# A mask of scores as four 64x64 quarter products in place of 67-row products

## Chip, cores and metric

The kernel runs on one core of a Trainium2 chip. The metric is the device time in microseconds, as a median of several runs. A separate execution was recorded by the hardware profiler; all rows below come from it.

## What is computed

Three layers stand behind one another. The first is an attention with 2 batches, 8 heads, 768 positions and a head size of 64. Each query sees the keys less than 16 positions away and, with `log(32)` added to the score, 24 summaries, each the maximum of k (mean of v) over a block of 32 positions:

```python
scores_s = scale * einsum(q, k_sum) + log(32)
scores_l = where(abs(i - j) < 16, scale * q @ k.T, -1e9)
a = softmax(concat([scores_l, scores_s]))
x = a @ concat([v, v_sum])
```

The second is a gated layer: `h = relu(x @ w_in)`, a convolution of three taps along the positions, `h * sigmoid(conv) @ w_out`. The third normalises x and adds `relu(xn @ w_ch1) @ w_ch2` to it. The weights arrive as 64-bit floats and are narrowed on the chip into a high and a low part.

## The kernel before, in words

All work is cut into named steps (`plan.op`), 1850 of them. A long list at the head of the file (`ORDER`) gives the order in which they are issued and the engine of each; each engine works through its own steps in that order, so a step that waits holds up what stands behind it on its engine.

The attention goes by pairs of blocks of 64 queries: `pair(j)`, j from 0 to 11, six per batch. A pair holds 8 heads as two units u = 2j and 2j + 1 (heads in the lower and the upper half of the partitions). Each unit has one PSUM bank of 128 queries (two blocks of 64) by four heads by 120 keys: 24 summaries and a window of 96 positions (16 ahead of the block, its 64, 16 behind it). The steps of a pair in order:

- `M{u}` (L460 to L466) takes a bank and writes the additive mask into it, as a product of `mask_l` and `mask_r`, with 480 columns (four heads of 120). `mask_l` (L293) holds the identity of 64 rows twice side by side, and three rows of ones; `mask_r` (L303) holds 64 rows of window masks in three variants (first block of a batch, middle, last block) and three rows that add up to `log(32)` under the summaries. Where both blocks of the pair use the same variant, it is one product of 67 rows by 128 queries; otherwise two of 67 rows by 64 queries.
- `S{j}` (L468 to L476) adds the scores: 32 products of 64x64 tiles with 120 columns, for four heads p, two units a and two blocks h_.
- `X`, `E`, `Q`, `R`, `N` (maximum, exponential, reciprocal, scaling), `P` (transposes back), `C` (copy) and `T` (product with the windows of v, L480). `H` and `L` split the result into high and low parts for the next layer.

Banks of the attention come from a ring of five. The steps `h` (L704) and `x` (L778) are the second layer, `ch` (L1114) and `ac` (L1149) the third; from about 49 us on the steps of the second layer stand among the pairs of the attention.

On TensorE the order around the masks is M1, M3, M0, S0, M2, S1 for pairs 0 and 1; then M4, M5, S2; M7, M6, S3; M9, M8, S4; M10, M11, S5; M15, M13, M14, M12, S6, S7; M17, M16, S8; M19, M18, S9; M20, M21, S10; M23, M22, S11. Between the masks of one pair no other step of TensorE stands, but for pairs 0 and 1 and pairs 6 and 7, which are interleaved as shown.

On GpSimd the order at the start is: `mhalf` (L319), `mask_r`, the identity `ident` (L282, used by every transpose and by the first steps of TensorE at L358), a clearing of `kw` (L322) and of `vw` (L594), `ind` (L284), a clearing of `xT`, `mask_l`, and then copies of k (L395). All loads go through one queue, SyncE's.

Of the kernel before, what the change touches and what calls it, by code (L numbers as in the profile page):

```python
# [100 lines left out]
F32 = mybir.dt.float32  # L101
F32R = mybir.dt.float32r
U32 = mybir.dt.uint32
BF16 = mybir.dt.bfloat16
AF = mybir.ActivationFunctionType
ALU = mybir.AluOpType
# [3 lines left out]
NEG = -1e9  # L110
F64_SCALE = 2.0 ** -112
F64_SIGN = -(2.0 ** 32)
LN32 = (3.46875, -0.003021240234375, 7.152557373046875e-06)
# [48 lines left out]
def local_summary_attention_moe_kernel(  # L162
# [26 lines left out]
    NB = S // 32  # L189
    HK = 16  # L190
    WN = 15
    K0 = NB + HK
    K1 = K0 + 64
    NK = K1 + HK
    SCALE = 1.0 / float(D) ** 0.5

    V, A, G, T = nc.vector, nc.scalar, nc.gpsimd, nc.tensor
# [7 lines left out]
    def pool(name, bufs=1, space=None, side="left"):  # L205
        kw = {} if space is None else {"space": space}
        return tc.alloc_tile_pool(name=name, bufs=bufs, side=side, **kw)

    const = pool("const")
# [4 lines left out]
    ps_a = pool("ps_a", space=PSUM, side="right")  # L214

    ident = const.tile([128, 128], F32, name="ident")
    mask_l = const.tile([67, 128], BF16, name="mask_l")
    mask_r = const.tile([67, 3, NK], BF16, name="mask_r")
    crow = const.tile([28, 128], F32, name="crow")
    ccol = const.tile([128, 28], F32, name="ccol")  # L220
    mhalf = const.tile([128, NT], F32, name="mhalf")
# [28 lines left out]
    def scaled(e, out, in_, c=None):  # L250
        if e == "A":
            A.copy(out, in_) if c is None else A.mul(out, in_, c)  # L252
        elif c is None:
            on[e].tensor_copy(out, in_)
        else:
            on[e].tensor_scalar(out=out, in0=in_, scalar1=c, scalar2=1.0, op0=ALU.mult, op1=ALU.mult)  # L256
# [3 lines left out]
    def bank(tag):  # L260
        p, n = PS[tag]
        return p.tile([128, 512], F32, tag=tag, name=tag, bufs=n)
# [27 lines left out]

    ind_op = plan.op("ind", (("G", 640),), make_ind)

    def make_mask_l(e):  # L293
        G.memset(mask_l[0:64], 0.0)
        G.affine_select(
            out=mask_l[0:64].rearrange("p (a j) -> p a j", a=2),
            in_=mask_l[0:64].rearrange("p (a j) -> p a j", a=2),
            compare_op=ALU.not_equal, fill=1.0, base=0,
            pattern=[[0, 2], [-1, 64]], channel_multiplier=1,
        )  # L300
        G.memset(mask_l[64:67], 1.0)

    def make_mask_r(e):  # L303
        G.memset(mask_r, 0.0)
        loc = mask_r[0:64, :, NB:NK]
        G.affine_select(out=loc, in_=loc, compare_op=ALU.is_ge, fill=NEG, base=WN - HK,
                        pattern=[[0, 3], [1, NK - NB]], channel_multiplier=-1)
        G.affine_select(out=loc, in_=loc, compare_op=ALU.is_ge, fill=NEG, base=HK + WN,
                        pattern=[[0, 3], [-1, NK - NB]], channel_multiplier=1)
        G.memset(mask_r[0:64, 0, NB:K0], NEG)  # L310
        G.memset(mask_r[0:64, 2, K1:NK], NEG)
        ln = mask_r[64:67, :, 0:NB]
        G.memset(ln, LN32[0])
        for i in (0, 1):
            G.affine_select(out=ln, in_=ln, compare_op=ALU.is_ge, fill=LN32[i + 1], base=i,
                            pattern=[[0, 3], [0, NB]], channel_multiplier=-1)

    masks = [plan.op("mask_l", (("G", 600),), make_mask_l), plan.op("mask_r", (("G", 2354),), make_mask_r)]
    G.memset(mhalf, -0.5)  # L319
    kz = {}  # L320
# [108 lines left out]
    live = {}  # L429
# [13 lines left out]
    def pair(j):  # L443


        n, half = divmod(j, 2)
        c = n % NCH
        ws = (2 * half, 2 * half + 1)
        waits = KE[n] + [KC[n], KH[n]] + QE[n] + ([kz[n % 3]] if n % 3 in kz else [])
        if half == 0 and c > 0:  # L450
            waits.append(KX[n])
        if half == 1 and c < NCH - 1:
            waits.append(KX[n + 1])
        var = [0 if (c == 0 and w == 0) else 2 if (c == NCH - 1 and w == NW - 1) else 1 for w in ws]
        ms, cs = [], []
        for a in range(2):
            u = 2 * j + a
            tag = "tr"

            def f_m(e, u=u, tag=tag):  # L460
                sc = live["sc", u] = bank(tag)
                for h_ in range(1 if var[0] == var[1] else 2):
                    s_ = slice(0, 128) if var[0] == var[1] else slice(64 * h_, 64 * h_ + 64)
                    T.matmul(sc[s_, 0:4 * NK].rearrange("p (a c) -> p a c", a=4), mask_l[:, s_],
                             mask_r[:, var[h_]].unsqueeze(1).to_broadcast([67, 4, NK]), start=True, stop=False)
            ms.append(plan.op(f"M{u}", (("P", 200),), f_m, masks, take=[(tag, ("s", u))]))  # L466

        def f_s(e):  # L468
            for p in range(4):
                for a in range(2):  # L470
                    for h_ in range(2):
                        T.matmul(live["sc", 2 * j + a][64 * h_:64 * h_ + 64, p * NK:(p + 1) * NK],  # L472
                                 qb[n % 2][64 * a:64 * a + 64, p, ws[h_], :], kw[n % 3][64 * a:64 * a + 64, p, ws[h_], :],
                                 start=False, stop=(p == 3))

        s = S_[j] = plan.op(f"S{j}", (("P", 950),), f_s, waits + ms)  # L476
        for a in range(2):
            cs.append(unit(2 * j + a, s))

        def f_av(e):  # L480
            av = live["av", j] = bank("tr")
            ps = [live.pop(("ps", 2 * j + a)) for a in range(2)]
            for h_ in range(2):
                vv = vw[j % 3][0:NK, h_, :].rearrange("p (h e) -> p h e", h=4)
                for p in range(4):
                    for a in range(2):
                        s_ = slice(64 * a, 64 * a + 64)
                        T.matmul(av[s_, h_ * 256 + p * 64:h_ * 256 + p * 64 + 64], vv[:, p, s_],  # L488
                                 ps[a][:, p, 64 * h_:64 * h_ + 64], start=True, stop=True)

        tt = T_[j] = plan.op(f"T{j}", (("P", 1090),), f_av, cs + [LV[j], LVS[j]], take=[("tr", ("av", j))])
        for a in range(2):
            tt.give.append(("probT", 2 * j + a))
        if half == 0:
            def f_new(e):
                t = xTT[n] = m1.tile([128, 2, 4, CH + 2], F32R, tag="xT", name="xT", bufs=2)
                xT[n] = [t[:, k_] for k_ in range(2)]
                if c == 0:
                    G.memset(t[:, :, :, 0:1].bitcast(F32), 0.0)
                if c == NCH - 1:  # L500
                    G.memset(t[:, :, :, CH + 1:CH + 2].bitcast(F32), 0.0)
            XT[n] = plan.op(f"xT{n}", (("G", 100),), f_new, [], take=[("xT", n)])
        o = 1 + 128 * half
        av_ = lambda: live["av", j].rearrange("p (w h j) -> p h w j", w=2, h=4)
        to = lambda x: x[:, :, o:o + 128].rearrange("p h (w j) -> p h w j", w=2)
        XH[j] = plan.op(f"H{j}", EVAC, lambda e: scaled(e, to(xT[n][0]), av_()), [tt, XT[n]])

        def f_lo(e):
            hi, lo = xT[n]
            V.tensor_tensor(out=to(lo), in0=av_(), in1=to(hi).bitcast(F32), op=ALU.subtract)  # L510

        XL[j] = plan.op(f"L{j}", (("V", 598),), f_lo, [XH[j]])
        XL[j].give.append(("tr", ("av", j)))
        if half == 0 and c > 0:
            def f_halo(e):
                u_, d_ = xTT[n - 1], xTT[n]
                scaled(e, u_[:, :, :, CH + 1:CH + 2], d_[:, :, :, 1:2])
                scaled(e, d_[:, :, :, 0:1], u_[:, :, :, CH:CH + 1])
            HL[n] = plan.op(f"xh{n}", (("V", 200), ("G", 470)), f_halo, [XL[j], XL[j - 1]])
# [166 lines left out]
    def m_step(i):  # L686
# [84 lines left out]
        for t in range(2):  # L771
# [10 lines left out]
            if f == NF - 1:  # L782
                def fe(e, t=t):
# [10 lines left out]
                                                   in_=conv_w.rearrange("k (f p) -> (k f) p", p=256))),  # L794
# [464 lines left out]
```

## Time and profile before

| | |
|---|---|
| median of 3 runs | 496.11 us (495.74 to 496.38) |
| profiled execution, whole time | 497.45 us |
| its span, first to last instruction | 495.6 us |
| TensorE busy | 478.3 us (96%) |
| VectorE, ScalarE, GpSimd busy | 303.6, 227.7, 143.5 us |
| mask products at L464 | 32 |

The profiled execution is one of its own, with a whole time a little above its span; a sum made against it is carried over to the median of the runs as a difference. Engine names in the rows are PE (TensorE matmul), PEld (its weight loads), DVE (VectorE), ACT (ScalarE), POOL (GpSimd) and SPq (SyncE's issue of loads). A matmul's listed duration contains the filling and emptying of the array, so the pace of a run of products is read from one start to the next, not from single durations. An engine's idle time is named after what ended it, in brackets behind an arrow.

### The profile page before, as it was taken

What the parts mean: (1) busy time and instruction counts of PE and PEld (TensorE: products, weight loads), DVE (VectorE), ACT (ScalarE), POOL (GpSimd) and SP (SyncE); (2) the same over time, 40 slices, a digit from 0 to 9 for tenths busy, and PEclk for the clock granted to TensorE, in tenths of its full rate; (3) what the DMA queues carried; (4) which work ended last, traced back from release to release, by engine and by line L of the source; (5) the groups of instructions that cost most, each with busy time, mean ns of one, the idle gap of its engine ahead of it and who ended that gap; (6) DMA issues with size and microseconds to landing.
All of it is one profiled execution on the core that took longest, in us unless ns stands there. A gap on an engine that the chain in (4) does not pass through costs nothing.

```text
span 495.6 us, 8628 instructions
## 1 busy us (share of the span) xinstructions
PE 478.3 (96%) x3342; PEld 415.8 (84%) x3342; DVE 303.6 (61%) x601; ACT 227.7 (46%) x605; POOL 143.5 (29%) x177
## 2 busy tenths in 40 slices
PE   6886999999999999999999999999999999999997
PEld 4545989888888888887889989899899888989985
DVE  3888999889867898999899751304551012301114
ACT  3888986674856587745443412314342010110100
POOL 5554565554233364325323102222422000000000
PEclk9898999999999999999999999999999999999999
DMA  8999997213100423000450402113240001200003
GB/s 267 346 246 232 212 238 157 48 24 65 32 1 0 136 85 123 0 1 25 147 170 1 169 1 69 51 51 115 64 161 1 0 1 44 82 3 2 0 1 127
DMA packets 60196, 43.35 MB, mean 87 GB/s; under 512 B 34336, under 2 KB 55100, under 8 KB 60156
## 3 DMA queue, kind: packets, MB, share of 16 engines
q1 hardware_dynamic: 60012, 42.68, 30.8%
q8 instruction: 26, 0.43, 0.4%
q14 instruction: 14, 0.11, 0.1%
q10 hardware_dynamic: 144, 0.13, 0.1%
HBM read 39.22 MB, written 3.15 MB: 85 GB/s over the span
## 4 chain that ended last, share of the span: by engine, by line
PE 71%; DMA 8%; issue 7%; DVE 4%; POOL 4%; ACT 3%; SPq 3%; DVEq 0%; POOLq 0%; ACTq 0%
PE ch L1114 21%; PE acc L1149 20%; PE x L778 11%; PE h L704 10%; DMA raw<-in_moe_w_ch_dram 4%; POOL wl L644 3%; PE tr L488 2%; PE tr L472 2%; PE tr L566 1%; DMA wst<-in_moe_w_in_dram 1%; DMA wst<-in_moe_w_out_dram 1%; PE x L823 1%; PE tr L351 1%; SPq L331 1%; DVE c L734 1%
## 5 line engine op out<-in xcount | busy, mean ns | idle before, releaser
L1149 PE MATMUL acc<-wh,ch 128*128 128x512 f32 x382 | 126.2, 394 | 1.2 <-ACT x2b L252 0.7
L1125 DVE SCALAR_TENSOR_TENSOR ch<-ch,ch 128x384 fp32r<-128x384 f32 x64 | 35.4, 556 | 133.8 <-ACT ch L1121 133.6
L1121 ACT ACTIVATE ch<-ch 128x384 fp32r<-128x384 f32 x64 | 31.3, 490 | 154.5 <-PE ch L1114 113.2
L1114 PE MATMUL ch<-xnT,wh 128*128 128x384 f32 x512 | 100.0, 337 | 0.0
L1114 PEld LDWEIGHTS ch<-xnT,wh 128*128 128x128 f32 x512 | 90.6, 188 | 4.2 <-DVE ch L1125 0.6
L1149 PEld LDWEIGHTS acc<-wh,ch 128*128 128x128 f32 x382 | 71.6, 188 | 17.1 <-ACT x2b L252 1.1
L644 POOL TENSOR_TENSOR wl<-raw,wh 128x512 fp32r<-128x512 f32 x32 | 43.9, 1388 | 112.5 <-ACT wh L642 101.1
L1149 PE MATMUL acc<-wl,ch 128*128 128x512 f32 x191 | 75.1, 393 | 0.0
L704 PE MATMUL h<-xT,wi 128*128 128x258 f32 x504 | 72.1, 287 | 0.4 <-ACT h L716 0.4
L704 PEld LDWEIGHTS h<-xT,wi 128*128 128x128 f32 x504 | 65.7, 189 | 6.8 <-ACT h L716 4.3
L778 PE MATMUL x<-wo,ghi 128*128 128x512 f32 x192 | 61.6, 402 | 0.0
L765 POOL TENSOR_TENSOR glo<-g,ghi 128x256 fp32r<-128x256 f32 x48 | 39.2, 821 | 71.5 <-ACT ghi L758 56.8
L734 DVE SCALAR_TENSOR_TENSOR c<-h,ccol,c 128x256 f32<-128x256 f32 x96 | 56.2, 604 | 3.1 <-POOL c L256 1.2
L1114 PE MATMUL ch<-xnT,wl 128*128 128x384 f32 x256 | 54.9, 336 | 0.0
L1114 PEld LDWEIGHTS ch<-xnT,wl 128*128 128x128 f32 x256 | 45.3, 188 | 0.0
L1149 PEld LDWEIGHTS acc<-wl,ch 128*128 128x128 f32 x191 | 35.8, 188 | 6.7
L778 PE MATMUL x<-wo,glo 128*128 128x512 f32 x96 | 38.1, 397 | 0.1
L1084 DVE STREAM_TRANSPOSE xf<-xn 32x384 f32<-32x384 f32 x64 | 36.5, 570 | 1.3
L778 PEld LDWEIGHTS x<-wo,ghi 128*128 128x128 f32 x192 | 32.2, 189 | 4.0 <-ACT ghi L758 0.3
L537 ACT ACTIVATE prob<-tr,nm 128x120 f32<-128x120 f32 x96 | 33.2, 368 | 3.4 <-DVE nm L525 2.9
L642 ACT CAST wh<-raw 128x512 fp32r<-128x512 f32 x32 | 20.3, 659 | 23.0 <-PE acc L1149 13.5
L739 ACT ACTIVATE c<-c 128x256 f32<-128x256 f32 x48 | 19.7, 418 | 14.8 <-DVE c L734 14.6
(131 smaller groups left out, 592.8 us busy)
## 6 DMA issues: line engine op xcount, KB each, us to landing
raw<-in_moe_w_ch_dram SPq DMA_DIRECT2D x32, 512.0 KB, 5.5
wst<-in_moe_w_out_dram SPq DMA_DIRECT2D x8, 512.0 KB, 6.3
vw<-in_v_dram SPq DMA_DIRECT2D x20, 192.0 KB, 6.1
wst<-in_moe_w_in_dram SPq DMA_DIRECT2D x5, 512.0 KB, 5.1
s_q<-in_q_dram SPq DMA_DIRECT2D x8, 256.0 KB, 4.1
early<-in_k_dram SPq DMA_DIRECT2D x3, 512.0 KB
x2a<-in_moe_w_in_dram SPq DMA_DIRECT2D x3, 512.0 KB
early<-in_v_dram SPq DMA_DIRECT2D x3, 512.0 KB, 9.1
```

The costliest lines, as they stand in the source:

```text
L537: A.activation(out=pr[:, p, :], in_=sc[:, p * NK:(p + 1) * NK], func=AF.Exp, bias=nm[:, p:p + 1], scale=1.0, accum_out=sm[:, p:p + 1])
L642: d = plan.op(name + "d", (("A", 520),), lambda e: A.copy(hi(), narrowed(raw())), [c_] + list(extra))
L644: lambda e: G.tensor_tensor(out=lo(), in0=narrowed(raw()), in1=hi().bitcast(F32), op=ALU.subtract),
L704: T.matmul(live["h", i][:, 0:CH + 2], w_[:, c, f * 128:(f + 1) * 128], x_[:, c, :], start=(k_ == 0 and c == 0), stop=(k_ == 2 and c == 3))
L734: V.scalar_tensor_tensor(out=ct, in0=ht[:, kk:kk + CH], scalar=ccol[:, kk * NF + f:kk * NF + f + 1], in1=ct, op0=ALU.mult, op1=ALU.add)
L765: on[e].tensor_tensor(out=glo, in0=live.pop(("g", i)), in1=live["ghi", i].bitcast(F32), op=ALU.subtract)
L778: T.matmul(x2ps[g, t], l[:, ts_], r[:, f, :], start=(f == 0 and j == 0), stop=(f == NF - 1 and j == 2))
L1084: V.transpose(out=o_, in_=i_)
L1114: T.matmul(cp[:, 0:384], w_[:, c * 128:(c + 1) * 128], x_[:, c, s], start=(n_ == 0), stop=(n_ == 11))
L1121: A.activation(out=chs[b, m][0][:, s], in_=live[key][:, 0:384], func=AF.Relu)
L1125: V.scalar_tensor_tensor(out=lo[:, s], in0=live.pop(key)[:, 0:384], scalar=0.0, in1=hi[:, s].bitcast(F32), op0=ALU.max, op1=ALU.subtract)
L1149: T.matmul(acc[key], l[:, ts_], r[:, 512:1024], start=(mm == 0 and j == 0), stop=(done and j == 2))
```

## The change

Both mask tables now have 64 rows and stand twice, in partitions 0 to 63 and 64 to 127. Each query picks four neighbouring rows (cyclically) instead of one row and three rows of ones: of any four neighbours the summary columns add up to `log(32)`, since the rows hold its three parts and a zero in turn (`ln_c`), and the window masks of four neighbours together block what lies outside the window. GpSimd builds the tables with more steps than before. The first of a pair's two `M` steps to come only takes its bank; the second issues the products for both units: four of 64x64 tiles, with unit a_ on row half a_ and block h_ on column half h_, always with 480 columns.

```diff
-    mask_l = const.tile([67, 128], BF16, name="mask_l")
-    mask_r = const.tile([67, 3, NK], BF16, name="mask_r")
+    mask_l = const.tile([128, 128], BF16, name="mask_l")
+    mask_r = const.tile([128, 3, NK], BF16, name="mask_r")
+    ln_c = const.tile([64, 16], F32, name="ln_c")
...
     def make_mask_l(e):
-        G.memset(mask_l[0:64], 0.0)
-        G.affine_select(
-            out=mask_l[0:64].rearrange("p (a j) -> p a j", a=2),
-            in_=mask_l[0:64].rearrange("p (a j) -> p a j", a=2),
-            compare_op=ALU.not_equal, fill=1.0, base=0,
-            pattern=[[0, 2], [-1, 64]], channel_multiplier=1,
-        )
-        G.memset(mask_l[64:67], 1.0)
+        G.memset(mask_l[0:64], 1.0)
+        ml = mask_l[0:64].rearrange("p (a j) -> p a j", a=2)
+        for sign, base, fill in ((-1, 3, 0.0), (1, 0, 0.0), (1, 60, 1.0)):
+            G.affine_select(out=ml, in_=ml, compare_op=ALU.is_ge, fill=fill, base=base,
+                            pattern=[[0, 2], [-sign, 64]], channel_multiplier=sign)
+        G.tensor_copy(mask_l[64:128], mask_l[0:64])
 
     def make_mask_r(e):
-        G.memset(mask_r, 0.0)
+        G.memset(ln_c, 0.0)
+        for i in range(3):
+            G.affine_select(out=ln_c, in_=ln_c, compare_op=ALU.not_equal, fill=LN32[i], base=-i,
+                            pattern=[[-4, 16]], channel_multiplier=1)
+        n_ = 8
+        while n_:
+            G.tensor_tensor(out=ln_c[:, 0:n_], in0=ln_c[:, 0:n_], in1=ln_c[:, n_:2 * n_], op=ALU.add)
+            n_ //= 2
+        G.memset(mask_r[0:64], 0.0)
         loc = mask_r[0:64, :, NB:NK]
-        G.affine_select(out=loc, in_=loc, compare_op=ALU.is_ge, fill=NEG, base=WN - HK,
+        G.affine_select(out=loc, in_=loc, compare_op=ALU.is_ge, fill=NEG, base=2,
                         pattern=[[0, 3], [1, NK - NB]], channel_multiplier=-1)
         G.affine_select(out=loc, in_=loc, compare_op=ALU.is_ge, fill=NEG, base=HK + WN,
                         pattern=[[0, 3], [-1, NK - NB]], channel_multiplier=1)
+        G.affine_select(out=loc[0:3], in_=loc[0:3], compare_op=ALU.is_ge, fill=0.0, base=61,
+                        pattern=[[0, 3], [-1, NK - NB]], channel_multiplier=1)
         G.memset(mask_r[0:64, 0, NB:K0], NEG)
         G.memset(mask_r[0:64, 2, K1:NK], NEG)
-        ln = mask_r[64:67, :, 0:NB]
-        G.memset(ln, LN32[0])
-        for i in (0, 1):
-            G.affine_select(out=ln, in_=ln, compare_op=ALU.is_ge, fill=LN32[i + 1], base=i,
-                            pattern=[[0, 3], [0, NB]], channel_multiplier=-1)
+        G.tensor_copy(mask_r[0:64, :, 0:NB], ln_c[:, 0:1].unsqueeze(2).to_broadcast([64, 3, NB]))
+        G.tensor_copy(mask_r[64:128], mask_r[0:64])
...
             def f_m(e, u=u, tag=tag):
-                sc = live["sc", u] = bank(tag)
-                for h_ in range(1 if var[0] == var[1] else 2):
-                    s_ = slice(0, 128) if var[0] == var[1] else slice(64 * h_, 64 * h_ + 64)
-                    T.matmul(sc[s_, 0:4 * NK].rearrange("p (a c) -> p a c", a=4), mask_l[:, s_],
-                             mask_r[:, var[h_]].unsqueeze(1).to_broadcast([67, 4, NK]), start=True, stop=False)
+                live["sc", u] = bank(tag)
+                if ("sc", u ^ 1) not in live:
+                    return
+                for a_ in range(2):
+                    for h_ in range(2):
+                        k_, s_ = slice(64 * a_, 64 * a_ + 64), slice(64 * h_, 64 * h_ + 64)
+                        T.matmul(live["sc", 2 * j + a_][s_, 0:4 * NK].rearrange("p (a c) -> p a c", a=4), mask_l[k_, s_],
+                                 mask_r[k_, var[h_]].unsqueeze(1).to_broadcast([64, 4, NK]), start=True, stop=False)
```

## Rows read from the trace of the kernel before

**Rows 1.** The page: TensorE's busy time, and the granted clock in 40 slices.

```profile
PE 478.3 (96%) x3342; PEld 415.8 (84%) x3342; DVE 303.6 (61%) x601; ACT 227.7 (46%) x605; POOL 143.5 (29%) x177
...
PEclk9898999999999999999999999999999999999999
```

**Rows 2.** Busy time by stage: stage in us, its length, engines with instruction counts.

```profile
core 0: us, PE busy (x) PEld busy (x) DVE busy (x) ACT busy (x) POOL busy (x), PEclk, DMA share, GB/s
...
60.00:80.00 20.00, 19.86 (x177) 17.23 (x176) 19.73 (x33) 16.66 (x43) 12.68 (x14) 1.00 0.96 219
80.00:100.00 20.00, 20.00 (x192) 17.67 (x191) 17.86 (x46) 14.26 (x45) 10.61 (x18) 1.00 0.35 70
...
288.00:488.00 200.00, 200.00 (x1009) 181.10 (x1008) 49.87 (x90) 40.40 (x76) 21.25 (x16) 1.00 0.12 40
```

**Rows 3.** TensorE's waits, before 60 us and after: total us, times, longest.

```profile
PE tr L566 <- POOL prob L556: 2.7, 1, 2.7
...
PE tr L488 <- DMA vw<-in_v_dram: 1.3, 2, 0.8
...
PE acc L1149 <- ACT x2b L252: 0.7, 1, 0.7
PE acc L1149 <- DVE ch L1125: 0.5, 1, 0.5
PE h L704 <- ACT h L716: 0.4, 1, 0.4
```

**Rows 4.** The chain that ended last, pieces in order of time: start, length.

```profile
53.75 6.79 DMA wst<-in_moe_w_out_dram
...
65.41 0.63 PE tr L566 x4
...
186.24 0.72 PE x L778 x3
```

**Rows 5.** TensorE's timeline at three places of the masks: start, length, instruction, count.

```profile
17.23 1.01 PE L464 MATMUL tr<-mask_r,mask_l 67*64 67x480 bf16 x5
...
92.94 0.60 PE L351 MATMUL tr<-ident,s_q 128*128 128x128 f32 x4
93.38 1.32 PE L464 MATMUL tr<-mask_r,mask_l 67*128 67x480 bf16 x6
94.63 1.87 PE L472 MATMUL tr<-kw,qb 64*64 64x120 f32 x64
...
108.76 0.57 PE L464 MATMUL tr<-mask_r,mask_l 67*128 67x480 bf16 x2
109.26 1.05 PE L472 MATMUL tr<-kw,qb 64*64 64x120 f32 x32
...
145.57 0.60 PE L464 MATMUL tr<-mask_r,mask_l 67*64 67x480 bf16 x4
146.09 1.05 PE L472 MATMUL tr<-kw,qb 64*64 64x120 f32 x32
```

**Rows 6.** Timeline of the start, with idle time ahead and its releaser in brackets.

```profile
2.81 0.68 POOL L315 TENSOR_SCALAR_AFFINE_SELECT mask_r<-mask_r 3x72 bf16<-3x72 bf16 x2
...
3.83 0.29 POOL masks.py:199 TENSOR_SCALAR_AFFINE_SELECT ident<-ident 128x128 f32<-128x128 f32 x1
...
5.88 1.09 PE L358 MATMUL x<-ident,early 128*64 128x128 f32 x16 [2.09 <-DMA early<-in_k_dram]
...
37.42 0.43 DVE L623 TENSOR_SCALAR wst<-wst 128x512 uint32<-128x512 uint32 x1 [0.72 <-DMA wst<-in_moe_w_out_dram]
```

**Rows 7.** GpSimd's groups by line and form: busy us, mean ns, idle before.

```profile
L1027 POOL TENSOR_TENSOR rs<-rs,mhalf 128x6 f32<-128x6 f32 x2 | 2.9, 1440 | 0.6 <-DVE rs L1024 0.6
...
L254 POOL COPY kw<-ksum 128x384 f32<-128x384 f32 x2 | 1.3, 630 | 0.0
...
L254 POOL COPY kw<-kw 128x64 f32<-128x64 f32 x2 | 0.6, 328 | 0.0
...
L286 POOL TENSOR_SCALAR_AFFINE_SELECT ind<-ind 128x40 f32<-128x40 f32 x1 | 0.2, 220 | 0.1
```

## The prediction

> **What bounds the kernel now.** I read the page's engine table first: TensorE is busy 96% of the span, and its granted clock shows the digit 9 in every slice of 12.4 us but the second and the fourth, where an 8 says that part of the slice ran at the lower of the two levels (1.2 in place of 2.4 GHz) [rows 1]. Then the stages: from 60 to 80 us TensorE is busy 19.86 of 20 us, but VectorE 19.73; from 80 us TensorE is full and VectorE has room (17.86 of 20); from 288 us on TensorE runs alone [rows 2]. Then TensorE's waits: up to 60 us it waits for others (2.7 us for GpSimd's normalised scores, 1.3 us for v windows still on their way, the larger two shown), after 60 us only 1.6 us in three places [rows 3]. Last the chain that ended last: at 53.75 us it lies in a weight load of 6.79 us, from 65.41 us to the piece at 186.24 us every piece is TensorE [rows 4]. So a microsecond of TensorE's work is worth a microsecond after 65 us, and little before, where loads set the pace.
>
> **The change part by part.**
>
> *The mask products, TensorE.* There are 12 pairs of blocks. I price a product wave w and a change of tile shape s from two rows: at 108.76 us two whole-array products of 480 columns lead to the scores' products (64x64 tiles) 0.50 us later, so 2w + s = 0.50. At 93.38 us six products stand: whole, two halves, whole, two halves, with the scores 1.25 us later [rows 5]. Four half products take 0.52 us at 145.57 us, as long as two whole ones, so two halves (67 rows by 64 columns) run side by side and the six are four waves, each followed by a change of shape: 4(w + s) = 1.25. Hence w = 0.19 and s = 0.12 us.
>
> After the change each pair has four products, one in each quarter. Nothing in the trace shows a 64-row mask product, so the bounds are: all four at once (one wave), or two waves. The nearest row is the scores themselves, the same four quarters in the same order with two data sets per row half: 64 of them in 1.87 us, 29 ns each, where a whole-array float32 product of 128 columns takes 110 ns (four from 92.94 to 93.38 us), 103 ns for 120 columns [rows 5]. 103 / 29 is 3.5 at once, so I take one wave.
>
> The change of shape moves: it was between mask and scores, and is now ahead of the mask, whose quarters have the shape of the scores. So a plain pair costs s + w = 0.31 in place of 0.50, a gain of 0.19. The two pairs at 93.38 us have both masks behind one another (the first of each pair's two steps now issues nothing): s + 2w = 0.50 for 1.25, a gain of 0.75. The pair at 145.57 us gains 0.52 - 0.31 = 0.21. After 65 us that is 0.75 + 3 x 0.19 (108.76 us and two like it at 121.84 and 129.60 us) + 0.21 = 1.5 us. At two waves per pair it is 1.25 - (0.12 + 0.76) = 0.37 at 93.38 us and nothing elsewhere.
>
> Here stands a rule that speaks against the change. The row says that products in the same row half overlap: the scores' order is (row half 0, column half 0), (0, 1), (1, 0), (1, 1), and 3.5 run at once [rows 5]. The Trainium skill's page "TensorE: Matmul & The Clock Gate", Part 3, Packing small matmuls, The mechanism, states that a weight load overlaps a running product only where the row group differs; by that the second quarter would wait for the first, and the sum would be the two-wave one. The trace speaks against it; what it would make is the second rival.
>
> *Before 65 us.* Six pairs: five products at 17.23 us in 1.01 us [rows 5] become s + w = 0.31, the next pair's remaining product loses its change of shape (0.12), four plain pairs gain 0.19 each: together 0.70 + 0.12 + 0.76 = 1.6 us. I count them at nothing: TensorE then waits longer for the same v windows and scores [rows 3], and whatever the later of these pairs gain ends at the work behind the weight load that lands at 60.55 us (53.75 + 6.79 [rows 4]), with VectorE full right after it [rows 2]. If that cover is gone, they are worth up to 1.6 us.
>
> *The later place of a pair's first mask.* The second step now writes both banks, so it needs both free. Behind it in TensorE's queue stand that pair's scores, which need both anyway. In 17 to 22 us unit 3's mask moves behind the first pair's scores, ahead of its own. No mask row waits for a bank now [rows 5], so nothing is charged, and since no wait stands there, none can be gained either; a loss would show as an idle time ahead of the masks.
>
> *The table, GpSimd.* It comes first in GpSimd's queue, ahead of the identity that TensorE's first transposes need. Removed: two selects of 3x72, 0.68 us [rows 6], and a small memset. Added: three selects on 64x16 at most 0.22 each, 0.66; four additions of 8 columns or fewer, seen nowhere: low end 0.33 each by a copy of 128x64, high end 1.44 by the power over 128x6 [rows 7]; I take 0.33, because an addition is nearer a copy than a power, 1.3; a select of 3x288, some 0.4, between 0.34 (3x72) and 0.63 (128x384 copy); two copies, 0.33 and 0.63; a memset, at most 0.2 [rows 6, 7]. Sum 3.5 - 0.7 = 2.8 us more, up to 7.3 at the high end. The other table (mask_l) adds two selects and a copy less a memset, some 0.7 us, behind the identity and 11 us before its first use at 17.23 us [rows 5]: free.
>
> The identity is ready at 3.83 + 0.29 = 4.12 us and TensorE starts at 5.88 us, when k arrives [rows 6]. At 6.9 us it starts 1.0 us late. ScalarE and VectorE follow, but at 37.42 us VectorE waits 0.72 us for a weight load [rows 6], and TensorE behind it 1.3 us for v windows [rows 3]; the queue of loads does not depend on these transposes. So I cost 1.0 us at nothing. At the high end the start is 5.5 us late, and cover of 0.72 + 1.3 = 2.0 leaves 3.5 us.
>
> *DMAs:* none added, removed or moved. The weight loads of the last stage, released by the attention's last step, go out earlier with it.
>
> *Sum.* -1.5 us on a span of 495.6, 494.1; that execution took 497.45 us as a whole, the median of the runs is 496.11, so the forecast is 496.11 - 1.5 = **494.6 us**. What is gained by 146 us must last to the end: the links behind 187 us, where TensorE waits 1.6 us in all [rows 3], start from TensorE's own work at 186.24 us [rows 4], so they shift with it.
>
> **Rivals.**
>
> *Absorbed.* TensorE gains, and waits for VectorE or ScalarE instead, right behind the masks or in the three waits shown [rows 3]. For it: VectorE is nearly full at 60 to 80 us. Against: it has 2 us in 20 to spare afterwards [rows 2], and the chain holds no other engine up to 187 us. Time about 496.1.
>
> *Two waves*, by whatever keeps quarters of one row half apart, or a change that does less than it says: gain 0.4, 495.7. Against: 3.5 scores at once.
>
> *Early gains count too*: 1.5 + 1.6, 493.0. Against: the load at 53.75 us.
>
> *Slower: the identity is late.* GpSimd's four small additions cost like the power row; TensorE's start is 5.5 us late, 3.5 remain after the cover, less 1.5 gained: +2.0, 498.1. It decides once the build is longer by more than 1.76 (the slack to 5.88 us) + 2.0 + 1.5 = 5.3 us. For it: GpSimd has the identity behind the table. Against: every row of plain arithmetic or copying over so few columns.
>
> **How the numbers follow.** Forecast 0.55; early gains too 0.08; absorbed 0.17; two waves 0.10; late identity 0.10. Under 0.2% (1.0 us, about what a measurement of this kernel can tell) fall absorbed, two waves and a little of the forecast where a third of its gain is lost: 0.30. Faster 0.60, slower 0.10. The range goes from 492.9, all pairs gaining, to 496.8, which takes in the two cases near no change with 0.7 us for a start that is partly uncovered; the late identity lies beyond.
>
> **What would show it.** In the profile after: 48 mask products of 64x64 tiles; from the first mask to the first score some 0.2 us in a plain pair (the change of shape now lies ahead) and 0.4 us at 93 us, in place of 0.50 and 1.25; TensorE busy some 2 to 3 us less; the identity ready near 7 us and the first transpose right behind it; VectorE's wait at 37 us shorter, the start of the unbroken TensorE stretch near 65 us as before; the last score 1.5 us sooner than now. Wrong if 0.4 us or more stands between the first mask and the scores of a plain pair, if an addition on GpSimd takes over 1 us, or if the waits of TensorE after 65 us grow by the gain.

## The result and the profile after

| | before | after |
|---|---|---|
| median of 6 runs, same chip | 496.38 us (495.74 to 497.84) | 499.50 us (498.53 to 500.96) |
| profiled execution, whole time | 497.45 us | 499.72 us |
| its span | 495.6 us | 498.0 us |

The ratio of after to before is 1.0052, with a 95% interval of 1.0032 to 1.0072: the change makes the kernel 3.1 us **slower**, where 1.5 us faster was forecast.

The page of the changed kernel, to be held against [rows 1]: busy time of the engines and the granted clock.

```profile
PE 477.5 (96%) x3358; PEld 418.3 (84%) x3358; DVE 303.1 (61%) x601; ACT 227.7 (46%) x605; POOL 146.0 (29%) x187
...
PEclk9997999999999999999999999999999999999999
```

There are sixteen products more and ten instructions more on GpSimd, as the diff says, and TensorE's busy time is 0.8 us less (2 to 3 were named as a sign). Nothing here says slower. The masks themselves, in TensorE's timeline of the changed kernel (start, length, instruction, count), against [rows 5]:

```profile
96.00 0.60 PE L359 MATMUL tr<-ident,s_q 128*128 128x128 f32 x4
96.52 0.60 PE L475 MATMUL tr<-mask_r,mask_l 64*64 64x480 bf16 x8
96.95 1.81 PE L483 MATMUL tr<-kw,qb 64*64 64x120 f32 x64
...
110.76 0.60 PE L359 MATMUL tr<-ident,s_q 128*128 128x128 f32 x4
111.29 0.40 PE L475 MATMUL tr<-mask_r,mask_l 64*64 64x480 bf16 x4
111.52 0.99 PE L483 MATMUL tr<-kw,qb 64*64 64x120 f32 x32
...
147.21 0.40 PE L475 MATMUL tr<-mask_r,mask_l 64*64 64x480 bf16 x4
147.43 0.99 PE L483 MATMUL tr<-kw,qb 64*64 64x120 f32 x32
```

The masks do what was forecast: from the first mask to the first score 0.23 and 0.22 us in a plain pair (before 0.50 and 0.52), 0.43 us in the double one (before 1.25). But everything is late: the scores start at 96.95 us where they started at 94.63 us. This lateness gets smaller from mask to mask: 2.32 us here, 2.26 at 111.52 us, 1.34 at 147.43 us. So the loss lies ahead of the masks, and the place to look is the stretch in which loads set the pace. The same view at the instruction that stood at 65.41 us [rows 4] shows it already 3.05 us late:

```profile
68.46 0.60 PE L577 MATMUL tr<-ident,prob 128*120 128x128 f32 x4
```

Then TensorE's waits after 60 us in the changed kernel (total us, times, longest), against [rows 3]; no wait has taken the place of the gain:

```profile
PE acc L1160 <- ACT x2b L253: 0.7, 1, 0.7
PE h L715 <- ACT h L727: 0.4, 1, 0.4
PE acc L1160 <- DVE ch L1136: 0.2, 1, 0.2
```

Further back, pieces of the chain that ended last in the changed kernel (start, length, what), up to where it becomes TensorE alone:

```profile
16.12 4.25 SPq L339
...
20.41 2.71 SPq L339
...
23.24 6.98 DMA wst<-in_moe_w_in_dram
...
40.50 4.19 DMA vw<-in_v_dram
...
44.83 1.98 PE tr L499 x32
```

The end hangs on the queue of loads here too: SyncE is held at the early v loads (line 339) until 23.12 us, and only then does a load of w_in go out. The timeline of SyncE's queue in the kernel before (start, length of the group, line, tile):

```profile
13.89 6.98 SPq L331 DMA_DIRECT2D early<-in_v_dram  x3
...
20.99 3.03 SPq L661 DMA_DIRECT2D wst<-in_moe_w_in_dram  x2
...
37.04 3.07 SPq L601 DMA_DIRECT2D vw<-in_v_dram  x4
```

and in the changed kernel:

```profile
15.00 8.12 SPq L339 DMA_DIRECT2D early<-in_v_dram  x3
...
23.24 3.22 SPq L672 DMA_DIRECT2D wst<-in_moe_w_in_dram  x2
...
40.50 3.15 SPq L612 DMA_DIRECT2D vw<-in_v_dram  x4
```

The same loads of the same size are issued 1.1, 2.3 and 3.5 us later: the queue falls further behind with each of these groups. The busy time by stage tells why. For each stretch its length, the engines with their instruction counts, the granted clock, the DMA engines' busy share (the time that packets took over the engines' time; it can pass 1) and GB/s; first the kernel before:

```profile
8.00:12.00 4.00, 2.84 (x48) 2.60 (x48) 2.62 (x6) 2.64 (x6) 1.17 (x3) 1.00 1.13 360
12.00:16.00 4.00, 3.35 (x59) 3.32 (x61) 3.78 (x11) 2.24 (x5) 2.17 (x5) 1.00 1.11 372
```

then the changed one:

```profile
8.00:12.00 4.00, 4.00 (x68) 3.94 (x64) 2.31 (x5) 1.63 (x3) 1.50 (x5) 1.00 1.14 312
12.00:16.00 4.00, 2.23 (x39) 2.02 (x37) 3.77 (x10) 2.21 (x5) 2.07 (x3) 1.00 1.15 301
```

The last two columns are the finding of the study: the DMA engines are as busy as before (1.14 and 1.15 for 1.13 and 1.11) and move less, 312 GB/s for 360 and 301 for 372. They don't wait more; their packets take longer. Nothing in the diff mentions a load. What it does touch is the tile `ln_c`: 64 bytes per partition, put among the constants, at the head of SBUF. By the allocation of the tiles, everything behind it on that side of SBUF moves up by 64 bytes, the landing places of the first loads (`early`, `wst`, `x2a`) among them; in the kernel before these all lie on multiples of 256 bytes. The attention's tiles (`vw`, `s_k`, `s_q`) are laid out from the other end and stay where they were.

### The profile page after: what moved, and what is told of

Read it like the earlier page. It is cut to its first block, busy times and chain, and to the rows that moved or that the text cites. A ratio compares the mean times of both kernels' runs of the same rounds, so it can differ in the third digit from the quotient of the medians.

```text
span 498.0 us, 8671 instructions
## 1 busy us (share of the span) xinstructions
PE 477.5 (96%) x3358; PEld 418.3 (84%) x3358; DVE 303.1 (61%) x601; ACT 227.7 (46%) x605; POOL 146.0 (29%) x187
## 4 chain that ended last, share of the span: by engine, by line
PE 71%; DMA 7%; issue 6%; DVE 5%; SPq 5%; POOL 4%; ACT 3%; DVEq 0%; POOLq 0%; ACTq 0%
PE ch L1125 21%; PE acc L1160 20%; PE x L789 10%; PE h L715 10%; DMA raw<-in_moe_w_ch_dram 4%; POOL wl L655 3%; SPq L339 3%; PE tr L499 3%; PE tr L577 2%; PE tr L715 2%; DVE c L745 2%; PE tr L359 1%; DMA wst<-in_moe_w_in_dram 1%; PE tr L483 1%; SPq L672 1%
```

## The experiments

The first four runs belong to the theory of the late identity, the first suspect; the next four tested the place of the tiles against it; the last four asked which moves matter, and whether more tiles can gain. Each ratio is to the kernel before, run beside it on the same chip, with its 95% interval.

### e1_ident_first: the identity built first

```diff
-ORDER = """ 5G 0V 8S 6V 11S ... 52V 2G 53A 54V ...
+ORDER = """ 2G 0V 8S 6V 11S ... 52V 5G 53A 54V ...
```

(In the changed kernel; step 2 is the identity, step 5 `mask_r`.)

> The changed kernel with two steps of GpSimd exchanged: the identity is built first, the mask table where the identity was. Theory A, the longer table holds back the identity and with it TensorE's first transposes, at a lower granted clock, and all that hangs on them: the first transpose starts at 5.9 us when k lands, its sixteen take 1.1 us in place of 1.98, and the time falls to 493.5 to 495.5 us, below the kernel before, since the masks' gain of about 2 us is left. Theory B, the loss does not come from the identity but from the loads being slower or from the moved mask products: 498 us or more, as the changed kernel.

Measured: 500.26 us, ratio 1.0073 (1.0044 to 1.0102). The identity is out of the way (the first transposes start at 5.56 us, their sixteen still take 1.98 us) and the time is no better. The loads are as slow as in the changed kernel, in the same view as above:

```profile
12.00:16.00 4.00, 2.78 (x49) 2.75 (x51) 3.75 (x10) 2.23 (x5) 2.16 (x4) 1.00 1.15 301
```

### e2_before_late: the kernel before with an unused ln_c

```diff
+    ln_c = const.tile([64, 16], F32, name="ln_c")
...
     def make_mask_r(e):
+        G.memset(ln_c, 0.0)
+        for i in range(3):
+            G.affine_select(out=ln_c, in_=ln_c, compare_op=ALU.not_equal, fill=LN32[i], base=-i,
+                            pattern=[[-4, 16]], channel_multiplier=1)
+        n_ = 8
+        while n_:
+            G.tensor_tensor(out=ln_c[:, 0:n_], in0=ln_c[:, 0:n_], in1=ln_c[:, n_:2 * n_], op=ALU.add)
+            n_ //= 2
```

> The kernel before with one part of the change alone: the summary column of eight instructions on GpSimd (a memset, three selects, four additions, 1.93 us) is built ahead of the mask table, and not used. Theory A: the identity is ready at about 6.05 us in place of 4.12, and the time rises by 2.5 to 4.5 us, to 498.9 to 500.9. Theory B: TensorE starts 0.3 us late and the loads cover it: 496 to 496.8.

Measured: 499.74 us, ratio 1.0073 (1.0045 to 1.0101). Alone, this looks like the proof of the late identity: more work ahead of it, and slower by as much as the change. But TensorE starts at 5.86 us, no later than before (5.88 us [rows 6]), as its timeline shows (idle time ahead and its releaser in brackets):

```profile
5.86 1.97 PE L367 MATMUL x<-ident,early 128*64 128x128 f32 x16 [2.08 <-POOL ident masks.py:199]
```

The edit brought two things, eight instructions and 64 bytes. Its loads moved 300 GB/s from 12 to 16 us. It doesn't tell the two apart; e5 does.

### e3_before_first: the kernel before, identity first

The edit of e1, in the kernel before.

> The kernel before with the identity built first and the mask table in its place. Control: k lands at 5.88 us, after the identity in either order, so both theories expect no change, 495.4 to 496.8 us. A gain of 1 us or more would say that the identity's place was already worth something before the change.

Measured: 496.72 us, ratio 1.0006 (0.9988 to 1.0025). No difference; the identity's place is worth nothing there either. Its loads moved 371 GB/s from 12 to 16 us.

### e4_warm11: more products ahead of the first transposes

```diff
-        for _ in range(6):
+        for _ in range(11):
```

(The first products of TensorE, on a tile of their own, in the changed kernel.)

> The changed kernel with 11 in place of 6 warm-up products on TensorE, which then is busy up to 6 us. Theory A with the lower clock as the main part: the sixteen first transposes take 1.1 us in place of 1.98 and the time falls by 1 to 2 us, to 497.5 to 498.5. Theory A with the lateness as the main part, or theory B: less than 0.5 us, 499 to 500.

Measured: 499.14 us, ratio 1.0062 (1.0038 to 1.0087). The changed kernel's first sixteen transposes took 1.98 us where they took 1.09 us before [rows 6], at the lower level of the clock: the clock records of its trace show the full level from 8.99 us on, those of before from 4.40 us. With eleven products ahead the sixteen take 1.09 us again, and the time stays where it was. The clock at the start isn't the cause.

### e5_before_pad64: nothing but a moved place

```diff
+    const.tile([128, 16], F32, name="pad")
```

(In the kernel before, where the change has its `ln_c`. No instruction is added or changed.)

> The kernel before, no instruction changed: only an unused tile of 64 bytes per partition stands where the change puts ln_c, so that the landing places of the early loads (x2a, wst, early) and the tiles behind them lie 64 bytes higher. Theory C, the loss comes from these places, since loads into them run slower (300 in place of 370 GB/s from 12 to 16 us in every slow run so far): 498.5 to 500.5 us, with the same low rate. Theory A, it comes from GpSimd's longer table: no change, 495.7 to 496.8 us, 370 GB/s.

Measured: 500.86 us, ratio 1.0088 (1.0065 to 1.0110), 4.0 us more than the 496.83 us of before beside it. An unused tile costs about as much as the whole change and its gain together, a little more than expected. Busy time by stage, from the same columns as above:

```profile
8.00:12.00 4.00, 4.00 (x62) 3.90 (x58) 2.65 (x6) 2.19 (x4) 0.63 (x2) 1.00 1.14 312
12.00:16.00 4.00, 2.76 (x50) 2.59 (x48) 3.75 (x10) 2.24 (x6) 2.07 (x3) 1.00 1.15 301
```

### e6_after_same_places: the change without a moved place

```diff
-    ln_c = const.tile([64, 16], F32, name="ln_c")
...
+    ln_c = ind[0:64, 0:16]
```

(The sums are worked out in `ind`, which is filled only later. All instructions of the change stay.)

> The changed kernel with ln_c laid into the first 64 bytes of ind, which is written later, so that every tile has the place it has before; all instructions stay. Theory C: 370 GB/s from 12 to 16 us, and 493.8 to 495.5 us, the masks' gain of 1.5 to 2 us without the loss. Theory A: 498.5 to 500 us, since the table holds back the identity as much as ever.

Measured: 495.63 us, ratio 0.9976 (0.9962 to 0.9990): **faster** than before by 1.2 us, and just above the expected range. The loads are back, by stage:

```profile
8.00:12.00 4.00, 4.00 (x60) 4.00 (x58) 2.26 (x5) 1.63 (x3) 1.54 (x6) 1.00 1.13 360
12.00:16.00 4.00, 2.61 (x47) 2.33 (x45) 3.77 (x9) 2.20 (x4) 2.07 (x3) 1.00 1.12 371
...
24.00:60.00 36.00, 29.86 (x394) 23.20 (x393) 33.19 (x68) 32.83 (x129) 20.55 (x21) 0.95 1.08 237
```

and the masks, in TensorE's timeline:

```profile
93.16 0.60 PE L475 MATMUL tr<-mask_r,mask_l 64*64 64x480 bf16 x8
93.58 1.81 PE L483 MATMUL tr<-kw,qb 64*64 64x120 f32 x64
...
143.85 0.40 PE L475 MATMUL tr<-mask_r,mask_l 64*64 64x480 bf16 x4
144.07 0.99 PE L483 MATMUL tr<-kw,qb 64*64 64x120 f32 x32
```

The scores are now 1.05 us sooner than before at the double pair and 2.02 us sooner at 144.07 us; the weight load that stood at 53.75 us [rows 4] starts at 53.43 us, so TensorE enters the stretch 0.32 us sooner. Between the two, the masks give 1.7 us, and in the changed kernel the lateness went down by as much, from 3.05 to 1.34 us.

Not all of it lasts. At 156 to 161 us TensorE's products for `h` lose 0.33 us again, in this trace and in the changed kernel's alike. TensorE's weight loads (PEld) for `h` wait for ScalarE's `h` there; their waits in the stretch of the masks (total us, times, longest), from 92 to 170 us before and in e6:

```profile
PEld h L704 <- ACT h L716: 1.8, 8, 0.3
...
PEld h L715 <- ACT h L727: 2.5, 9, 0.4
```

So 1.4 us is left at 170 us. The same sum, the matching products of TensorE held against the kernel before, gives 1.4 to 1.5 us between 92 and 170 us in every trace with the new masks.

### e7_after_pad128: moved by 128 bytes

```diff
     ln_c = const.tile([64, 16], F32, name="ln_c")
+    const.tile([128, 16], F32, name="pad")
```

> The changed kernel with 64 bytes more behind ln_c, so that the places move by 128 in place of 64 bytes. Theory C, if any move does it: as the changed kernel, 498.5 to 500. Theory C, if multiples of 128 bytes do not matter: 494 to 495.5 and 370 GB/s. Theory A: 498.5 to 500 us.

Measured: 499.42 us, ratio 1.0050 (1.0031 to 1.0070). By stage:

```profile
12.00:16.00 4.00, 3.45 (x61) 3.12 (x59) 3.68 (x10) 2.37 (x5) 2.15 (x4) 1.00 1.17 302
```

Twice the move costs the same. From 24 to 60 us its granted clock was 0.95, as in e6, where the changed kernel had 0.88 (its line first, then that of e7):

```profile
24.00:60.00 36.00, 29.03 (x379) 20.94 (x374) 29.95 (x60) 30.44 (x111) 19.03 (x20) 0.88 1.04 232
...
24.00:60.00 36.00, 29.34 (x397) 20.34 (x390) 32.70 (x62) 30.98 (x115) 19.75 (x20) 0.95 1.09 244
```

So that lower clock isn't what makes the changed kernel slow, though some of the 3.05 us by which its trace was late at 68.46 us may be the clock's.

### e8_same_places_first: same places and the identity first

The edits of e6 and e1 together.

> The run before last (places as before) with the identity built ahead of the table as well. Theory C with a share for A: up to 0.5 us below the kernel with the places alone, 493.3 to 495. Theory C alone: the same as that kernel within 0.3 us.

Measured: 496.75 us, ratio 0.9988 (0.9967 to 1.0009). Not told apart from e6, nor from the kernel before; there is no gain from an early identity, which the late-identity theory asks for.

### e9_after_pad256: moved by 256 bytes

```diff
     ln_c = const.tile([64, 16], F32, name="ln_c")
+    const.tile([128, 48], F32, name="pad")
```

> The changed kernel with 192 bytes behind ln_c, so that the places of the early loads move by 256 in place of 64 bytes. Theory C, places count by their remainder by 256: 360 to 372 GB/s from 8 to 16 us and 494 to 496 us, as with the places of before. Theory C', any move is bad: 310 GB/s and 498.5 to 500.

Measured: 496.32 us, 0.3 above the expected range, ratio 0.9981 (0.9953 to 1.0009). By stage:

```profile
12.00:16.00 4.00, 3.46 (x63) 3.18 (x61) 3.66 (x8) 2.42 (x4) 2.07 (x3) 1.00 1.11 371
```

The tile is back, and a second one beside it, and the loss is gone: what counts is the remainder of the places by 256 bytes, not that they moved.

### e11_before_pad256: the same in the kernel before

```diff
+    const.tile([128, 64], F32, name="pad")
```

> The kernel before with an unused tile of 256 bytes in place of the 64 tried earlier; no instruction changed. By 256-byte remainders: as the kernel before, within 0.2%, 360 to 372 GB/s from 8 to 16 us. If any move is bad: 499 to 501.

Measured: 497.06 us, ratio 1.0006 (0.9984 to 1.0029), with 373 GB/s from 12 to 16 us. An unused tile of 256 bytes costs nothing, one of 64 bytes 4.0 us.

### e10_at_places: the later landing places put on 256 bytes too

```diff
-    ln_c = const.tile([64, 16], F32, name="ln_c")
...
+    ln_c = ind[0:64, 0:16]
...
+        at.tile([128, 48], F32, name="pad0")
...
+                at.tile([128, 56], F32, name="pad1")
```

(The kernel of e6 with two unused tiles in the attention's pool. In the kernel before, `vw` lies 160 bytes and `s_k` and `s_q` lie 224 bytes past a multiple of 256; now all three lie on one. The attention's other tiles `kw`, `qb`, `vsum` and `parts` come onto one with them.)

> The changed kernel with the places of before, and in addition two unused tiles in the attention's pool, so that vw, s_k and s_q, whose places leave 160 and 224 bytes over multiples of 256, start at multiples of 256. If the rate of those loads hangs on the places as that of the early ones does, the loads from 24 to 60 us run at more than 235 GB/s, and the time falls by 0.5 to 2 us below the kernel with the places of before alone. If short rows are limited otherwise: the same within 0.3 us.

Measured: 493.49 us (492.27 to 495.50), ratio 0.9931 (0.9909 to 0.9953). This **beats both kernels**: 3.5 us less than the kernel before beside it, and against e6 a little more than expected (e12 below). By stage:

```profile
24.00:60.00 36.00, 31.47 (x406) 23.34 (x406) 34.83 (x74) 34.09 (x132) 21.00 (x22) 0.98 1.04 269
```

269 GB/s from 24 to 60 us where e6 had 237, at a lower busy share. SyncE's queue runs ahead, in its timeline:

```profile
48.98 0.47 SPq L676 DMA_DIRECT2D wst<-in_moe_w_out_dram  x1
```

That is the weight load which the kernel before issued at 53.75 us [rows 4] and on which its end hung; 4.8 us sooner, it is no longer in the chain that ended last, where every piece is TensorE's from 47.43 us up to 70 us (start, length, what):

```profile
47.43 1.71 PE h L716 x12
```

### e12_same_places_again: e6 once more, beside e10

> The changed kernel with ln_c in ind's bytes once more, timed beside the runs above. The masks' gain alone, by the trace 1.7 us between 65 and 146 us with the gain of the early pairs absorbed: a ratio of 0.995 to 0.998.

Measured: 495.73 us, ratio 0.9983 (0.9955 to 1.0011), as e6, and just above the expected ratios. So of e10's 3.5 us some 2.2 (495.73 - 493.49; 1.1 to 3.6 by the scatter of the two sets of twelve runs) come from the places in the attention's pool, and the rest from the masks. The clock isn't what e10 gains by: among the runs whose mean granted clock was 0.991 to 0.994, e10 has a median of 493.95 us (four runs) and e12 one of 495.87 us (seven).

### The packets

The time of a packet, worked out from the packets recorded in the traces: medians from 4 to 20 us for rows of 512 and 1024 bytes, means from 30 to 60 us for those of 256:

| kernel | places behind the constants | 512-byte rows | 1024-byte rows | 256-byte rows, mean |
|---|---|---|---|---|
| before | on 256 | 27 ns | 46 ns | 23.9 ns |
| after, e5 | 64 past | 32 ns | 51 ns | 23.0, 23.9 ns |
| e7 | 128 past | 32 ns | 51 ns | 23.7 ns |
| e6, e9, e11, e12 | on 256 | 27 ns | 46 ns | 23.6, 23.3, 21.9, 23.4 ns |
| e10 | on 256, `vw` and `s_q` too | 27 ns | 46 ns | 18.5 ns |

Packets that land off a multiple of 256 bytes take some 5 ns longer on average in these stretches, whether they are of 256, 512 or 1024 bytes and whether the place is 64, 128 or (in `vw` and `s_q`) 160 and 224 bytes past. It is not a fixed price on each: from 4 to 20 us over 99% of the 512-byte rows take 27 ns in the kernel before, and in the changed one 30% still do, while the slowest tenth takes 38 ns or more. For rows of 512 bytes 27 of 32 is 84% of the pace, and the bandwidth from 12 to 16 us fell to 301 / 372 = 81%.

Nor does a place off 256 always cost. The last layer's weights (`raw`) land 224 bytes past in every kernel here; after 100 us 84 to 87% of their 1024-byte rows take 46 ns, the time that such rows take on a multiple of 256 in the table, and from 235 to 236 us of the kernel before they moved 358 GB/s at a DMA share of 1.06. What sets these loads apart from the early ones, no run here shows.

The early loads can be held against a rule on the Trainium skill's page "DMA: Bandwidth & Descriptors", section "How a descriptor splits into AXI transactions": a descriptor is cut at multiples of 256 bytes, and one that starts off such a boundary fetches from the boundary below. Three things differ: the page tells it of reading, and here it is the place of landing that moved; by an estimate from its count of beats a 512-byte row would need 16, 18 and 20 of them at 0, 64 and 128 bytes past, where the runs show medians of 27, 32 and 32 ns; and by that count every such packet would take longer, `raw`'s too. Why the chip is slower on landing, no run here shows.

## Why the prediction was wrong, point by point

**The step that failed** is the one that had a single line: "*DMAs:* none added, removed or moved." None was added or removed, and none was issued in another order, but all landed elsewhere. The diff's first lines, a new tile among the constants, were priced at nothing without being named as an edit at all; the prediction costed the steps that write `ln_c` and not the 64 bytes that it takes. The moved places measured +4.0 us by themselves (e5; 3.2 to 5.5 us by its interval), against a gain of about 1.2 us (e6): 2.8 together, where +3.1 was measured. No rival held it. The range ended at 496.8 us because no bound in it came from the loads, though the prediction itself said that up to 65 us "loads set the pace" [rows 3, 4].

**The cover that wasn't.** Among the signs stood "the start of the unbroken TensorE stretch near 65 us as before", and it failed first: the instruction that stood there came 3.05 us late. That sign was well chosen; read alone, it sends the reader to the loads.

**The mask products: right.** One wave, not two. Forecast 0.2 and 0.4 us from first mask to first score; measured 0.22 to 0.23 and 0.43. The change of shape now stands ahead of the masks: from the four transposes to the mask 0.52 us (96.00 to 96.52) for 0.44 before [rows 5], so it costs 0.08 and not 0.12 there, and the wave 0.22 and not 0.19. The gain at the double pair is 1.25 - 0.43 - 0.08 = 0.74 us, forecast 0.75. Over the whole stretch the forecast was 1.5 us; 1.7 was measured up to the last masks in the traces of after and e6, and 1.4 is left at 170 us. e6's medians, 1.2 us less than before (0.5 to 1.9 by its interval), agree with it. The other three kernels with the new masks and places on 256 (e8, e9, e12) lie 0.1 to 0.2% below the kernel before, each with no change inside its interval: the gain is there in every trace, and only just clear of noise in the times.

The rule weighed against this, in the Trainium skill's "TensorE: Matmul & The Clock Gate", Part 3, The mechanism (a weight load overlaps only where the row group differs), isn't borne out: with four quarters, two of them in each row half, the first score starts 0.22 us after the first mask, and two waves of 0.19 would have been 0.38. The two-wave rival falls with it.

**Early gains: right to count at nothing.** In e6, where no late load hides them, TensorE enters the stretch only 0.32 us sooner of the 1.6 us that the earlier pairs gain; the weight load is the bound, as said. This is one execution, and the entry scatters: with the same remainders and masks it was 0.09 us sooner than before in e12's trace, 0.54 sooner in e8's and 1.61 later in e9's.

**The table and the late identity: right in kind, the price too high.** The timeline of GpSimd and TensorE at the changed kernel's start (idle time ahead in brackets):

```profile
1.82 1.00 POOL L311 TENSOR_TENSOR ln_c<-ln_c 64x8 f32<-64x8 f32 x4
...
5.96 0.29 POOL masks.py:199 TENSOR_SCALAR_AFFINE_SELECT ident<-ident 128x128 f32<-128x128 f32 x1
...
6.30 1.98 PE L366 MATMUL x<-ident,early 128*64 128x128 f32 x16 [2.51 <-POOL ident masks.py:199]
```

One of the four additions, among GpSimd's groups by form (busy us, mean ns, idle before):

```profile
L311 POOL TENSOR_TENSOR ln_c<-ln_c 64x8 f32<-64x8 f32 x1 | 0.2, 197 | 0.1
```

An addition took 0.2 us (forecast 0.33, high end 1.44), the identity was ready at 6.25 us (forecast 6.9) and TensorE started 0.42 us late (forecast 1.0). That this is hidden was right: e1, e3 and e8, with the identity first, gained nothing. **The slower rival**, 498.1 us from a late identity, came near the measured time by a mechanism that wasn't there.

**Absorbed** was wrong in the main: TensorE's waits after 60 us went from 1.6 to 1.3 us. In a small part it came true, in waits that this list doesn't have: the 0.33 us that go again at 156 to 161 us, where the weight loads for `h` wait for ScalarE (e6 above).

What stays open: why a landing place off 256 bytes costs 5 ns a packet here and nothing in `raw`'s loads; moves of other sizes than 64, 128 and 256 bytes; and what share of the loss is the landing places' alone, since every run that moves them moves other tiles too (in e5 also `wi`, `xT`, `h`, `c`, `g` and most weights of the last layer). For such a share there is a sign. The lateness of 1.34 us at 147 us and that of the span, 2.4 us, are 1.1 us apart. Of that 0.33 is what goes at 156 to 161 us (some 0.1 comes back before 300), and 0.4 comes after TensorE's last products; and between 300 and 490 us, where TensorE runs alone and waits for nothing, its same 956 products take longer, first before and then in the changed kernel:

```profile
300.00:490.00 190.00, 190.00 (x956) 171.78 (x955) 46.93 (x85) 38.92 (x73) 21.25 (x16) 1.00 0.13 43
...
301.50:491.90 190.40, 190.40 (x956) 172.04 (x955) 46.90 (x85) 38.90 (x73) 21.26 (x16) 1.00 0.13 43
```

From product to product it is 0.45 us, and it is no scatter: in all six traces with places 64 or 128 bytes past it lies between 0.44 and 0.75 us, and in all seven others on 256 it is 0.00. The weights loaded there land where they landed before, so this part isn't theirs; that TensorE reads tiles which moved is all that the record says of its cause.

## What to carry to other kernels

A new tile is an edit of every tile behind it: before pricing the instructions of a change, list the tiles that move and the loads that land in them, and try landing places on multiples of 256 bytes (64 unused bytes cost this kernel 0.9%, and putting the attention's tiles on 256 gained some 0.45%; `raw`, off 256, shows no loss). When GB/s falls at an unchanged DMA share, look at where and in what pieces the loads land, not at what they wait for. And an experiment that adds instructions on a new tile has two edits in it (e2): put the tile alone first (e5).

## What the runs showed of the hardware beyond that

Eight instructions more ahead of the identity cost TensorE 0.42 us at its start in the changed kernel and nothing in e2 (5.86 us for 5.88); by e1 and e8, where they stand behind it, they cost the kernel nothing. The sixteen first transposes at twice their time (1.98 for 1.09 us, in e1, e2 and e3 too) cost nothing either, by e4. Of what moved at the start, only the loads show in the time: from 4 to 20 us the changed kernel's moved 322 GB/s in place of 365, 12% less, and e5, with the same rates, was 4.0 us slower at the end. Between 24 and 60 us packets of 256 bytes at 18.5 ns in place of 23.4 (e10 and e12, means from 30 us on) went with 2.2 us gained.
